# A 48-chunk FFT, feed-forward and soft-MoE kernel: first two chunks replanned, spare products added, last part written in order

## The chip, the core and the metric

One core of a Trainium2 chip runs the whole program. The metric is the device time of one execution in microseconds; three runs of the kernel before took 1926.4 to 1935.65 us, with a median of 1929.36.

## What is computed

Three stages, on 8 batches of 3072 tokens with 256 channels:

```python
X = np.fft.rfft(x, axis=1)
Y = X * (filt_r + 1j * filt_i)[None, :, :]
x = np.fft.irfft(Y, n=3072, axis=1).reshape(24576, 256)
h = x @ w_in                              # 256 -> 2048, float64 weights
g = h * (1.0 / (1.0 + np.exp(-h)))
x = g @ w_out                             # 2048 -> 256, float64 weights
logits = x @ phi                          # 32 slots: 8 experts of 4
d = softmax(logits, over all tokens); slot_input = d.T @ x
slot_out[e] = np.maximum(slot_input[e] @ w1[e], 0) @ w2[e]
c = softmax(logits, over the slots);  out = c @ slot_out
```

## The kernel before, in words

The tokens are worked in 48 chunks of 512, six to a batch. A chunk's path: `mat4` (products py) ends the inverse transform, `out4` splits the result into two parts yT, `hidden` makes 16 tiles ph of six products each with the split weights w_hl, `act` applies silu into a tile g, `turn` transposes g on DVE into X, `logits` multiplies g with wp (w_out times phi, folded once) into pl, a running softmax follows (`soft0` to `soft3`), the exponentials go through DRAM (`spread0`, `spread1`) and `dsum` (pd) adds the chunk's weighted sums, which `update` folds into acc on DVE. There are 12 buffers for g, so a hidden tile needs the turn and the logits of the tile twelve before it.

The transform of a batch is four steps: stage one (pa, twelve pairs of rows, stored to DRAM scratch s1), four visits Q of stage two (gather a from s1, products px, scaling with the filter f on ACT, DVE and POOL) and of stage three (pb, copied to eb and stored to scratch s2), from which each chunk loads b (`load3`), and `fly` makes bp on DVE. Batch 0 does this alone at the start (`first_plan`, L407 on), the others between the hidden tiles of the batch before (`fft_plan`, L262 on).

The weights w_in and w_out come as float64 words and are decoded on the chip in quarters q of 512 columns: `dec_act` on ACT, `dec_dve` and `dec_low` on DVE, and for w_in `split_act` and `split_dve`, for w_out `dec_move` on ACT. Quarter q of w_in serves hidden tiles 4q to 4q+3. `make_wp` (pw) and `put_wp` fold a quarter of w_out with phi into four of the sixteen slices of wp.

The order of nearly all instructions on every engine is set by hand: each call is entered with a number, `at(t, fn, ...)`, and the calls are written out in the order of these numbers, one unit being a sixteenth of a chunk. In `first_plan` the numbers are given in microseconds, `us(t) = (t - T0) / 1.42`. The number decides order only; an instruction starts when its engine reaches it and its inputs are there. Every engine works its own list in order. All DMAs are issued by SP's queue. What follows the last chunk (from L879: merging the sums, the experts, the output) is left to a scheduler.

After the last chunk, the sums are merged (ptot, pn), turned (pnt), multiplied by w_out (psi, pT), sent through the experts (peh, pht, pso), and the slot outputs are spread over the tokens (po, copied to ots and stored). The weights of six of the eight experts are loaded meanwhile into buffers that the main loop gives back.

Of the kernel before, what the change touches and what calls it, by code (L numbers as in the profile page):

```python
# [9 lines left out]
F32 = mybir.dt.float32  # L10
# [20 lines left out]
T0 = 74  # L31

# [10 lines left out]
def fftconv_moe_softmoe(ctx, tc, x, cmat, chl, dmat, emat, gmat, filt, filt0, sign, w_in, w_outT, w_out,  # L43
# [129 lines left out]
    def fill_rest(b, Q):  # L173
        for g in range(2):
            DQ.dma_start(s1t[b][g, Q, :, :, NJ:S].rearrange("q u r e -> (q u) (r e)"),
                         filt[4:6, 0:16].rearrange("a p u c e -> p a (u c e)"))
# [85 lines left out]
    def fft_plan(b, t0):  # L262
# [7 lines left out]
        def load1(u):  # L270
            t = fp.tile([P, 2, CH], F32, tag="ld", bufs=BUFS["ld"], name=f"x_{b}_{u}")
            DQ.dma_start(t, pair(xb, u))
            c = fp.tile([P, 2, P] if b == 1 else [P, 2, 2, P], F32, tag="c", bufs=BUFS["c"], name=f"c_{b}_{u}")
            DQ.dma_start(c, (cmat if b == 1 else chl)[:, 2 * u:2 * u + 2])
            ld[u] = (t, c)
# [95 lines left out]

        if b == 1:
            t1, tx = [11.7 + 0.95 * u for u in range(12)], t0 + 27.1
        else:
            t1, tx = [t0 + d for d in (-4.3, -3.1, -1.9, -0.7, 2.6, 4.2, 6.4, 8, 11.5, 12.6, 13.7, 14.8)], t0 + 27.1
        at(t1[0] - 10, begin)
        if b == 1:
            for Q in range(4):
                at(8 + 2 * Q, fill_rest, 1, Q)
# [9 lines left out]
        tp = tx  # L389
        for Q in range(4):  # L390
            t = tx if Q == 0 else t0 + 16 * Q + VIS1 + 16
            at(t1[-1] + 4 if Q == 0 else tp + 2, load2, Q)
            at(t + 0.004, mat2, Q)
            for U in range(4):
                at(t - 6 + U, loadf, Q, U)
                at(t + ((1, 1.4, 2.4, 2.8) if Q == 0 else (1.75, 2.25, 4.15, 5.15))[U], act2, Q, U)
                at(t + (0.25, 0.65, 1.45, 2.05)[U], direct2, Q, U)
                at(t + ((1.4, 2, 3, 4) if Q == 0 else (2.25, 2.75, 5.15, 6.15))[U], cross2, Q, U)
                at(t + ((3.6, 3.7, 6, 6.1) if Q == 0 else (4.1, 4.2, 8.3, 8.4))[U], add2, Q, U)
            t = t0 + 16 * Q + VIS1 + 32  # L400
            at(t, mat3, Q)
            at(t + 0.001, out3, Q)
            at(t + 0.15, store3, Q)
            tp = t - 16 + 0.004 if Q else tx


    def first_plan():  # L407
# [10 lines left out]
        def load(v):  # L418
# [4 lines left out]
            DQ.dma_start(cs[v], cmat[:, 4 * v:4 * v + 4, :])  # L423
# [85 lines left out]

        at(us(-5), begin)  # L510
# [3 lines left out]
        at(us(-2.9), load_small)  # L514
        for u in range(12):
            t = 6 + u + (1 if u else 0)
# [3 lines left out]
        for u, n, t in ((0, 4, 13.4), (4, 4, 17), (8, 2, 18.9), (10, 2, 20.6)):  # L520
            at(us(t), store1, u, n)
        for Q in range(4):
            at(us((18, 18.1, 22.01, 22.41)[Q]), fill_rest, 0, Q)
            at(us(22 + 0.4 * Q), load2, Q)
            for U in range(4):
                at(us(22.05 + 0.4 * Q + 0.1 * U), loadf, 4 * Q + U)
            t = 28 + 4.8 * Q
# [14 lines left out]
        for q, (t0, t1, t2, t3, t4, t5, t6) in enumerate(((5, 21, 21.1, 21.15, 21.2, 21.3, 21.4), (39, 52.3, 52.4, 52.5, 53, 53.5, 54), (48.5, 54.1, 55, 56, 56.2, 57, 57.1), (53, 77.5, 79.2, 79.3, 80, 85, 85.2))):  # L542
            at(us(t0), load_words, "in", q)
            at(us(t1), dec_act, "in", q, "a" if q % 2 == 0 else "xh")
            at(us(t2), dec_dve, "in", q, 0)
            at(us(t3), dec_dve, "in", q, 1)
            at(us(t4), dec_low, "in", q)
            at(us(t5), split_act, q)
            at(us(t6), split_dve, q)
        at(us(62.6), load3, 0)  # L550
        at(us(68.5), fly, 0)
        at(us(66.1), start)
        for q, t in enumerate((81, 84.5, 89, 92)):
# [214 lines left out]

    tail = {"w1": [], "w2": [], "t": []}
# [66 lines left out]
    for c in range(NCHUNK):  # L836
        t0 = 16 * c
        if c > 0:
            at(t0 - 16 + 6.9, loadd, c)
            at(t0 - 16 + 5.6, load3, c)  # L840
            at(t0 - 16 + 9.6 if c > 1 else 15, fly, c)
        ty = t0 - 16 + (VIS3 + 0.003 if c > 1 else 15.7) if c else -2
# [3 lines left out]
        for m in range(NM):  # L846
# [16 lines left out]
        at(t3 + 0.001, update, c)  # L863
        if c % 4 == 3:
            last = c == NCHUNK - 1
            at(t3 + 4 if last else t1 + (11.2 if (c + 1) % CPB else 19.1), cprep, c // 4)
            if last:
                at(t1 + 0.5, exp_table)
                at(t3 + 5, cexp, c // 4)
                at(t3 + 6, cfin, c // 4)  # L870
            else:
                at(t1 + {1: 43.8, 3: 27.8, 5: 19.1}[(c + 2) % CPB], cfin, c // 4)
# [263 lines left out]
```

## Time and profile before

| what | value |
|---|---|
| median of three runs | 1929.36 us |
| profiled execution: its own time, and its span | 1931.86 us, 1930.1 us |
| PE busy, share of the span | 1817.5 us, 94% |
| DVE, ACT, POOL busy | 1258.0, 952.2, 264.5 us |
| mean granted clock of PE | 0.971 |
| bytes moved by DMA, mean rate | 292.67 MB, 152 GB/s |
| first product of chunk 0 (py), start | 80.53 us |
| first product of the output (po), start | 1862.62 us |

The span runs from the first to the last instruction. A busy PE is not a PE at its peak: the granted clock says at which share of 2.4 GHz it ran. In rows below, L62 is the helper that issues nearly all products, so tiles tell them apart.

### The profile page before, as it was taken

The numbers are of one execution on the slowest core, as the hardware profiler recorded it, in microseconds if no ns is written. First come the engines' busy times: TensorE is split into PE (matmuls) and PEld (weight loads), VectorE is DVE, ScalarE is ACT, GpSimd is POOL, SyncE is SP. The second block draws the span as 40 slices with busy tenths as digits, with TensorE's granted clock in tenths as the row PEclk, the third lists the DMA queues.
The fourth block names the chain that finished last, engine by engine and source line by source line (L and its number), as shares of the span: only waits on it lengthen the run. The fifth ranks groups of instructions, "written<-read, shape, count | busy, mean of one in ns | idle before, by whom it ended". The sixth has DMA issues, their size and how long they took to land. (4 is left out here: it accounts for less than half of the span.)

```text
span 1930.1 us, 49986 instructions
## 1 busy us (share of the span) xinstructions
PE 1817.5 (94%) x21250; PEld 1372.7 (71%) x21250; DVE 1258.0 (65%) x2170; ACT 952.2 (49%) x1785; POOL 264.5 (14%) x200
## 2 busy tenths in 40 slices
PE   4588999999999999999999999999999999999884
PEld 2366777877787777777787778777787777777543
DVE  4685675676676765676676766677576766765433
ACT  2443645545554545455455556456455454443322
POOL 0201211121121211121121212122022110000000
PEclk7798999999999999999999999999999999999987
DMA  9935525543344515543354415444355413122669
GB/s 307 367 113 176 156 69 160 175 141 109 117 159 147 168 51 167 175 133 120 115 161 156 153 47 180 162 134 135 101 172 173 126 63 102 68 83 76 228 233 386
DMA packets 237038, 292.67 MB, mean 152 GB/s; under 512 B 19344, under 2 KB 177424, under 8 KB 236816
## 3 DMA queue, kind: packets, MB, share of 16 engines
q1 hardware_dynamic: 236816, 289.49, 45.7%
q8 instruction: 167, 2.74, 0.6%
q14 instruction: 55, 0.45, 0.1%
HBM read 199.82 MB, written 91.68 MB: 151 GB/s over the span
## 5 line engine op out<-in xcount | busy, mean ns | idle before, releaser
L62 PE MATMUL ph<-yT,w_hl 128*128 128x512 f32 x4608 | 1100.6, 394 | 2.2 <-ACT g L631 1.8
L62 PEld LDWEIGHTS ph<-yT,w_hl 128*128 128x128 f32 x4608 | 853.2, 189 | 207.6 <-issue 26.6
L641 DVE STREAM_TRANSPOSE X<-g 128x512 f32<-128x512 f32 x768 | 516.7, 695 | 214.7 <-ACT g L631 211.0
L631 ACT ACTIVATE g<-ph 128x512 f32<-128x512 f32 x768 | 454.6, 608 | 342.2 <-PE ph L62 294.0
L239 POOL TENSOR_TENSOR sw<-sw,f 128x512 f32<-128x512 f32 x124 | 170.7, 1401 | 864.6 <-DVE X L641 487.2
L609 ACT ACTIVATE yT<-py 128x512 fp32r<-128x512 f32 x96 | 57.4, 598 | 352.6 <-PE py L62 352.6
L62 PE MATMUL pd<-X,E 32*32 32x512 f32 x6144 | 220.3, 603 | 0.0
L62 PEld LDWEIGHTS pl<-g,wp 128*32 128x32 f32 x6144 | 163.1, 110 | 74.3 <-issue 49.4
L62 PE MATMUL pl<-g,wp 128*32 128x128 f32 x6144 | 189.8, 275 | 6.8 <-issue 3.5
L62 PEld LDWEIGHTS pd<-X,E 32*32 32x32 f32 x6144 | 115.5, 103 | 78.2 <-issue 42.7
L725 DVE SCALAR_TENSOR_TENSOR acc<-acc,nm,pd 128x512 f32<-128x512 f32 x188 | 127.7, 741 | 51.3 <-PE pd L62 51.2
L284 POOL TENSOR_TENSOR xh<-x,xh 128x512 fp32r<-128x512 f32 x72 | 93.5, 1299 | 436.9 <-DVE xh L283 427.4
L610 DVE TENSOR_TENSOR yT<-py,yT 128x512 fp32r<-128x512 f32 x96 | 66.3, 691 | 67.3 <-ACT yT L609 67.3
L357 DVE TENSOR_TENSOR y<-y,sw 128x512 f32<-128x512 f32 x112 | 103.8, 966 | 0.0
L62 PE MATMUL py<-d,b 128*128 128x128 f32 x416 | 66.3, 283 | 18.0 <-DMA b<-s 14.4
L236 DVE TENSOR_TENSOR y<-px,f 128x512 f32<-128x512 f32 x120 | 78.0, 676 | 6.5 <-PE px L62 5.5
L228 ACT ACTIVATE sw<-px,sg 128x256 f32<-128x256 f32 x124 | 62.7, 505 | 37.5 <-DVE y L234 32.1
L671 ACT ACT_TABLE_LOAD x48 | 61.6, 1283 | 37.0 <-DVE nm L664 27.0
L62 PE MATMUL px<-a,em 24*32 24x512 f32 (+1 forms) x1072 | 50.1, 628 | 24.3 <-DMA a<-s 23.3
L367 ACT ACTIVATE eb<-pb 128x512 f32<-128x512 f32 x112 | 57.8, 602 | 27.8 <-PE pb L62 27.8
L62 PEld LDWEIGHTS py<-d,b 128*128 128x128 f32 x416 | 56.4, 197 | 20.8 <-DMA b<-s 15.3
L62 PE MATMUL py<-d,bp 128*128 128x128 f32 x352 | 60.2, 291 | 9.9 <-DVE bp L592 6.1
(142 smaller groups left out, 1196.3 us busy)
## 6 DMA issues: line engine op xcount, KB each, us to landing
a<-s SPq DMA_DIRECT2D x64, 512.0 KB, 5.1
f<-in_filt_dram SPq DMA_DIRECT2D x128, 256.0 KB, 4.0
s<-eb SPq DMA_DIRECT2D x64, 512.0 KB, 4.1
x<-in_x_dram SPq DMA_DIRECT2D x96, 256.0 KB, 3.8
b<-s SPq DMA_DIRECT2D x160, 128.0 KB, 3.1
out_dram<-ots SPq DMA_DIRECT2D x40, 512.0 KB, 5.4
c<-in_chl_dram SPq DMA_DIRECT2D x72, 256.0 KB, 3.7
s<-ea SPq DMA_DIRECT2D x56, 256.0 KB, 3.7
```

The source lines that it names most:

```text
L62: T.matmul(o, lhsT=l, rhs=r, start=start, stop=stop)
L228: A.activation(sw[:, 0, :], p[:, 1, :], AF.Copy, scale=sg[:, s:s + 1])
L236: V.tensor_tensor(y, p, f[:, 0, :].unsqueeze(1).to_broadcast([P, 2, CH]), op=ALU.mult)
L239: G.tensor_tensor(sw, sw, f[:, 1, :].unsqueeze(1).to_broadcast([P, 2, CH]), op=ALU.mult)
L284: G.tensor_tensor(h[:, 1, :], tf, h[:, 0, :], op=ALU.subtract)
L357: V.tensor_tensor(y, y, st.pop(("sw", Q, U)), op=ALU.add)
L367: A.activation(st["eb"][:, q], p, AF.Copy)
L610: V.tensor_tensor(y[:, half, 1, :], py, y[:, half, 0, :], op=ALU.subtract)
L631: A.activation(g, pht.pop((c, m)), AF.Silu)
L641: V.transpose(xt[c][:, m].rearrange("p b j -> p (b j)"), gt[c, m])
L671: A.activation(t[:, 0], L, AF.Exp, bias=nm[:, 1:2], accum_out=nm[:, 2:3])
L725: V.scalar_tensor_tensor(out=acc[:, :, a, :], in0=acc[:, :, a, :], scalar=mrun[c][:, 3:4], in1=p, op0=ALU.mult, op1=ALU.add)
```

## The change

- **First transfers.** The six loads of cmat for batch 0 are issued by ACT instead of SP. Two quarters of w_in (before: one) are loaded ahead of stage one's stores, the third ahead of the stores of stage three, the fourth behind the first load of b. Stage one of batch 0 is stored in three groups of four rows (before: 4, 4, 2, 2). The filling of unused scratch rows is one transfer per Q, and one for all of batch 1.
- **Decoding.** The second quarter of w_in is decoded during stage two of batch 0, and the others and w_out have new places. The turns of chunk 0 from tile 4 on move into the time of chunk 1, those of chunk 1 are a little later, and the logits of chunk 0 stand at tile 11.6.
- **Batch two.** Stage one of batch 1 is spread between tiles of chunk 1 (before: 0 and 1), and its visits of stage two and three move from 27.1, 33.9, 49.9, 65.9, 81.9 to 33.9, 44.4, 53.4, 65.9, 81.9 units; its c tiles are loaded in pairs.
- **Spare products.** `keep(n)` multiplies a 128x128 tile with itself n times into a PSUM tile that nothing reads: 12 before stage one, 72 after it, 44 after stage three (all on fold, zeroed first), 9 and then 1 to 4 at a time in the last part (on the identity).
- **Last part.** It is written in a fixed order in `finish`. The last chunk's sums are not folded into acc: they are copied to SBUF as part and multiplied with fs, and acc with fo (fs times the rescaling), into the same pn. Exp's table is loaded before the last logits, `cprep` and `cexp` stand behind sim, `cfin` behind the second expert tile, and the turns of hr run one tile ahead.

```diff
+W_IN = ((-2.8, 20), (-2.75, 27.5), (21.8, 56), (59.5, 72))
+W_OUT = ((61.1, 76.7), (61.12, 79.5), (61.3, 90.5), (61.4, 94.2))
...
+        v1 = [t0 + 16 * i + VIS1 for i in range(6)]
         if b == 1:
-            t1, tx = [11.7 + 0.95 * u for u in range(12)], t0 + 27.1
+            t1 = [16.2 + 0.87 * u for u in range(12)]
+            tx, tb = (v1[2], t0 + 44.4, t0 + 53.4, v1[4]), (t0 + 44.4, t0 + 53.4, v1[4], v1[5])
+            at(13, fill_rest, 1)
...
-            DQ.dma_start(cs[v], cmat[:, 4 * v:4 * v + 4, :])
+            A.dma_start(cs[v], cmat[:, 4 * v:4 * v + 4, :])
...
+        at(us(-5), V.memset, fold, 0.0)
+        at(us(-4.5), keep, 12, fold)
...
+        at(us(-2.7), fill_rest, 0, 0)
         for u in range(12):
-            t = 6 + u + (1 if u else 0)
+            t = 6 + u
             at(us(t), mat1, u)
             at(us(t + 1.2), out1, u)
             at(us(t + 2), sums1, u)
-        for u, n, t in ((0, 4, 13.4), (4, 4, 17), (8, 2, 18.9), (10, 2, 20.6)):
-            at(us(t), store1, u, n)
+            if u % 4 == 3:
+                at(us(t + 2.2), store1, u - 3, 4)
+        at(us(18.5), keep, 72, fold)
...
+            at(us(t0), load_words, "in", q)
+            at(us(t1), dec_act, "in", q, "a" if q % 2 == 0 else "xh")
+            at(us(t1 + 1.2), dec_dve, "in", q)
+            at(us(t1 + 4.6), dec_low, "in", q)
+            at(us(t1 + 7), split_act, q)
+            at(us(t1 + 8.2), split_dve, q)
+        at(us(60), keep, 44, fold)
...
+            at((11.5, 11.55, 17.75, 17.8)[q], make_wp, q)
+            at((11.51, 11.56, 17.76, 17.81)[q], put_wp, q)
...
+    def keep(n, a=None):
+        t = ps_h.tile([P, P], F32, tag="ph", name="keep")
+        a = idt if a is None else a
+        for _ in range(n):
+            mm(t, a, a, True, True)
...
-            at(max(t + 1.45 if m not in (1, 10) else t + 0.8996, 0 if c else 12 + 0.3 * m), turn, c, m)
+            at(max(t + 1.45 if m not in (1, 10) else t + 0.8996, (16.6 + 0.8 * (m - 4) if m > 3 else 11.7, 17.9 + 0.2 * m)[c] if c < 2 else 0), turn, c, m)
...
+        if c == NCHUNK - 1:
+            at(t1 + 0.0025, keep, 9)
...
+        fo = tp.tile([P, S], F32, tag="fo", name="fo")
+        V.tensor_scalar(fo, fs, nm[:, 3:4], None, op0=ALU.mult)
+        parts = []
+        for a, p in enumerate(pdt.pop(NCHUNK - 1)):
+            parts.append(wk.tile([P, NM, 32], F32, tag="g", bufs=BUFS["g"], name=f"part_{a}"))
+            if a % 2:
+                V.tensor_copy(parts[a], p)
+            else:
+                A.activation(parts[a], p, AF.Copy)
+        pn = ps_1.tile([P, 512], F32, tag="pl", name="pn")
+        for g in range(4):
+            mm(pn[S * g:S * g + S], fo, acc[:, 4 * g:4 * g + 4].rearrange("p m a j -> p (m a j)"), True, False)
+        keep(2)
+        for a in range(4):
+            for g in range(4):
+                mm(pn.rearrange("p (m a j) -> p m a j", a=4, j=32)[S * g:S * g + S, :, a, :], fs,
+                   parts[a][:, 4 * g:4 * g + 4], False, a == 3)
...
+        turn_hidden(0)
+        for i in range(4):
+            r, n = divmod(i, 2)
+            if i < 3:
+                turn_hidden(i + 1)
```

SP's queue after the loads of x for batch 0, before the change: words_in is a quarter of w_in, s<-a a store of stage one, s<-in_filt_dram a fill, a<-s the gather of stage two.

```order
L94 DMA words_in<-in_w_in_dram 128x1024 x2
L198 DMA s_0_88<-a_126 64x4x256 x8
L175 DMA s_0_88<-in_filt_dram 16x2x1024 x4
L198 DMA s_0_88<-a_126 64x2x256 x8
L202 DMA a_126<-s_0_88 128x4x256 x2
L175 DMA s_0_88<-in_filt_dram 16x2x1024 x2
L452 DMA f_0_235<-in_filt_dram 128x512
```

And in the changed kernel:

```order
L96 DMA words_in<-in_w_in_dram 128x1024 x4
L178 DMA s_0_89<-in_filt_dram 16x2x2048
L202 DMA s_0_89<-a_140 64x4x256 x12
L178 DMA s_0_89<-in_filt_dram 16x2x2048
L458 DMA f_0_306<-in_filt_dram 128x512
L227 DMA f_0_308<-in_filt_dram 128x256
L458 DMA f_1_310<-in_filt_dram 128x512
L206 DMA a_140<-s_0_89 128x4x256 x2
```

Twenty transfers of stores and fills stood between the words and the first gather, and now fourteen, with four loads of words and three filter loads around them.

SP's queue at the end of stage three of batch 0, before: s<-eb are its stores, b<-s the load of chunk 0, acc<-in_w_in_dram the fourth quarter of w_in.

```order
L567 DMA d_277<-in_dmat_dram 128x512
L260 DMA s_0_89<-eb_0_405 128x4x256 x2
L94 DMA words_in<-in_w_in_dram 128x1024 x2
L260 DMA s_0_89<-eb_1_491 128x4x256 x2
L260 DMA s_0_89<-eb_2_577 128x4x256 x2
L94 DMA words_in<-in_w_in_dram 128x1024 x2
L260 DMA s_0_89<-eb_3_626 128x4x256 x2
L94 DMA acc<-in_w_in_dram 128x1024 x2
L579 DMA b_656<-s_0_89 64x768 x2
L579 DMA b_656<-s_0_89 64x256 x2
L94 DMA a_126<-in_w_outT_dram 128x1024 x2
```

And now:

```order
L96 DMA words_in<-in_w_in_dram 128x1024 x2
L578 DMA d_358<-in_dmat_dram 128x512
L264 DMA s_0_90<-eb_0_498 128x4x256 x2
L264 DMA s_0_90<-eb_1_582 128x4x256 x2
L264 DMA s_0_90<-eb_2_668 128x4x256 x2
L264 DMA s_0_90<-eb_3_716 128x4x256 x2
L590 DMA b_729<-s_0_90 64x768 x2
L590 DMA b_729<-s_0_90 64x256 x2
L96 DMA acc<-in_w_in_dram 128x1024 x2
L96 DMA a_140<-in_w_outT_dram 128x1024 x8
```

No words of w_in stand between the stores of eb any more, and the fourth quarter has moved behind b.

ACT's list around the two copies of yT for chunk 0 (db_in<-... is `dec_act`, w_hl<-words_in is `split_act`), before:

```order
L105 ACTIVATE db_in_631<-words_in 128x1024
L131 ACTIVATE w_hl<-words_in 128x2x512
L105 ACTIVATE db_in_646<-words_in 128x1024
L131 ACTIVATE w_hl<-words_in 128x2x512
L609 ACTIVATE yT_685<-py_0_675 128x512
L609 ACTIVATE yT_685<-py_1_680 128x512
L631 ACT_TABLE_LOAD
L631 ACTIVATE g_0_697<-ph_0_690 128x512
L631 ACTIVATE g_1_708<-ph_1_699 128x512
L105 ACTIVATE db_in_717<-acc 128x1024
```

And now:

```order
L107 ACTIVATE db_in_723<-words_in 128x1024
L133 ACTIVATE w_hl<-words_in 128x2x512
L620 ACTIVATE yT_809<-py_0_799 128x512
L107 ACTIVATE db_in_812<-acc 128x1024
L620 ACTIVATE yT_809<-py_1_804 128x512
L642 ACT_TABLE_LOAD
L642 ACTIVATE g_0_828<-ph_0_821 128x512
L642 ACTIVATE g_1_839<-ph_1_830 128x512
L107 ACTIVATE db_out_841<-a_140 128x1024
L642 ACTIVATE g_2_854<-ph_2_843 128x512
L133 ACTIVATE w_hl<-acc 128x2x512
```

The decoding of the second and third quarters stood directly ahead of the first copy; now the fourth quarter's start stands between the two copies, and its split ahead of g of tile 3.

## Rows read from the trace of the kernel before

**Rows 1.** The page: busy time by engine, and granted clock in 40 slices.

```profile
PE 1817.5 (94%) x21250; PEld 1372.7 (71%) x21250; DVE 1258.0 (65%) x2170; ACT 952.2 (49%) x1785; POOL 264.5 (14%) x200
...
PEclk7798999999999999999999999999999999999987
```

**Rows 2.** Windows: length, busy by engine (instructions), granted clock, DMA share, GB/s.

```profile
0.00:10.00 10.00, 4.46 (x11) 3.55 (x12) 0.17 (x1) 2.35 (x3) 0.20 (x4) 1.00 0.71 226
10.00:20.00 10.00, 9.36 (x39) 6.82 (x37) 8.52 (x20) 4.44 (x10) 0.00 (x0) 1.00 1.07 374
20.00:30.00 10.00, 0.00 (x0) 0.00 (x0) 7.38 (x10) 2.54 (x3) 0.00 (x0) 0.71 0.93 318
30.00:40.00 10.00, 2.99 (x36) 1.25 (x38) 0.94 (x1) 0.00 (x0) 0.00 (x0) 0.50 0.77 256
80.00:90.00 10.00, 5.40 (x20) 4.46 (x20) 5.75 (x8) 2.82 (x4) 0.00 (x0) 0.54 0.96 334
90.00:194.00 104.00, 90.26 (x884) 68.74 (x898) 70.12 (x113) 46.13 (x78) 5.07 (x4) 0.92 0.49 157
```

**Rows 3.** Waits of PE: total us, times, longest.

```profile
PE py L62 <- DVE bp L592: 6.1, 2, 4.1
```

**Rows 4.** Timeline of SP's queue, first 100 us: start, us, line, transfers issued.

```profile
16.32 6.27 SPq L198 DMA_DIRECT2D s<-a  x8
...
25.76 5.27 SPq L198 DMA_DIRECT2D s<-a  x8
32.55 0.94 SPq L202 DMA_DIRECT2D a<-s  x2
...
67.62 1.39 SPq L260 DMA_DIRECT2D s<-eb  x2
...
75.67 3.19 SPq L579 DMA_DIRECT2D b<-s  x4
```

**Rows 5.** Timeline of PE, first 160 us: start, us, operation, records, idle before.

```profile
17.82 1.97 PE L62 MATMUL pa<-x,c 128*128 128x256 f32 x8 [0.22 <-DVE a L191]
36.59 1.03 PE L62 MATMUL px<-a,em 24*32 24x256 f32 x2 [16.80 <-DMA a<-s]
...
64.44 1.74 PE L62 MATMUL pb<-sw,gm 32*32 32x512 f32 x29
80.53 0.79 PE L62 MATMUL py<-d,b 128*128 128x128 f32 x2 [14.36 <-DMA b<-s]
...
90.25 15.71 PE L62 MATMUL ph<-yT,w_hl 128*128 128x512 f32 x68 [0.23 <-DVE yT L610]
...
159.40 4.49 PE L62 MATMUL pd<-X,E 32*32 32x512 f32 x128
```

**Rows 6.** Groups on DVE between 88 and 140 us: count, busy, mean ns.

```profile
L641 DVE STREAM_TRANSPOSE X<-g 128x512 f32<-128x512 f32 x17 | 11.1, 686 | 1.3 <-PE pw L62 1.3
L114 DVE SCALAR_TENSOR_TENSOR db_out<-a,db_out 128x1024 uint32<-128x1024 uint32 x4 | 4.9, 1226 | 0.1
```

**Rows 7.** Groups on ACT between 88 and 140 us: count, busy, mean ns.

```profile
L631 ACT ACTIVATE g<-ph 128x512 f32<-128x512 f32 x18 | 10.6, 602 | 10.3 <-PE ph L62 6.8 <-PE pl L62 2.9 <-issue 0.6
...
L128 ACT ACTIVATE a<-db_out 128x1024 f32<-128x1024 f32 x4 | 4.6, 1162 | 3.8 <-DVE db_out L114 3.8
```

**Rows 8.** Timeline of PE in the last part: start, us, operation.

```profile
1821.92 6.52 PE L62 MATMUL pd<-X,E 32*32 32x512 f32 x128
...
1834.68 4.23 PE L62 MATMUL psi<-wo,nT 128*32 128x256 f32 x32 [0.53 <-ACT nT L941]
...
1853.70 1.93 PE L62 MATMUL pso<-wt,hT 128*32 128x256 f32 x32 [0.25 <-ACT hT L974]
...
1862.62 7.79 PE L62 MATMUL po<-so,cl 32*128 32x256 f32 x104 [0.52 <-DVE so L983]
```

**Rows 9.** Timeline of DVE in the last part.

```profile
1828.28 2.72 DVE L725 SCALAR_TENSOR_TENSOR acc<-acc,nm,pd 128x512 f32<-128x512 f32 x4 [5.56 <-PE pd L62]
```

**Rows 10.** Timeline of ACT in the last part.

```profile
1818.13 1.28 ACT L671 ACT_TABLE_LOAD   x1 [0.77 <-DVE nm L664]
```

More of the change, by code (lines that the diff above doesn't have):

```diff
@@ L171, in scratch, with fill_rest @@
         return s1t[b % 2], s2t[b]
[L173 to L176, printed above, removed]
+    def fill_rest(b, Q=None):
+        to = s1t[b] if Q is None else s1t[b][:, Q:Q + 1]
+        n = 64 if Q is None else 16
+        DQ.dma_start(to[:, :, :, :, NJ:S].rearrange("g k q u r e -> (k q u) g (r e)"),
+                     filt[4:4 + n // 32 + 1].rearrange("a p u c e -> (a p u c e)")[0:n * 4096]
+                     .rearrange("(n g e) -> n g e", n=n, g=2))
     def pair(a, u):
@@ L840, in fftconv_moe_softmoe @@
             at(t0 - 16 + 5.6, load3, c)
[L841 to L842 removed]
+            at(t0 - 16 + 9.6 if c > 1 else 11.6, fly, c)
+        ty = t0 - 16 + (VIS3 + 0.003 if c > 1 else 14.9) if c else -2
         for h in range(2):
@@ L862, in fftconv_moe_softmoe @@
         at(t3, dsum, c)
-        at(t3 + 0.001, update, c)
+        if c < NCHUNK - 1:
+            at(t3 + 0.001, update, c)
         if c % 4 == 3:
             last = c == NCHUNK - 1
-            at(t3 + 4 if last else t1 + (11.2 if (c + 1) % CPB else 19.1), cprep, c // 4)
             if last:
-                at(t1 + 0.5, exp_table)
-                at(t3 + 5, cexp, c // 4)
-                at(t3 + 6, cfin, c // 4)
+                at(t0 + 16.95, exp_table)
             else:
+                at(t1 + (11.2 if (c + 1) % CPB else 19.1), cprep, c // 4)
                 at(t1 + {1: 43.8, 3: 27.8, 5: 19.1}[(c + 2) % CPB], cfin, c // 4)
@@ L906, in w2_of @@
-    def w2_of(e, k):
-        return w27[k // 2][:, k % 2, :] if e == 7 else w2t[e][:, k, :]
-    t = wk.tile([P, 16, TC], F32, tag="X", bufs=BUFS["X"], name="cl")
-    for k in range(NK - 2):
-        cl[k] = t[:, k, :]
-        DQ.dma_start(cl[k], cT[k])
-    nm = mrun[NCHUNK - 1]
-    mg = tp.tile([P, 8], F32, tag="mg", name="mg")
-    for a in range(4):
-        V.tensor_copy(mg[0:S, a:a + 1], nm[a * S:a * S + S, 0:1])
-    V.tensor_reduce(mg[0:S, 4:5], mg[0:S, 0:4], axis=AX.X, op=ALU.max)
@@ L929, in fftconv_moe_softmoe @@
-    V.tensor_scalar(fs, fold[:, 0:S], mg[:, 6:7], rec[:, 0:1], op0=ALU.mult, op1=ALU.mult)
-    pn = ps_h.tile([P, 512], F32, tag="ph", name="pn")
-    for g in range(4):
-        mm(pn[S * g:S * g + S], fs, acc[:, 4 * g:4 * g + 4].rearrange("p m a j -> p (m a j)"), True, True)
-    ns = wk.tile([P, 512], F32, tag="E4", bufs=BUFS["E4"], name="ns")
-    A.activation(ns[:, 0:256], pn[:, 0:256], AF.Copy)
-    V.tensor_copy(ns[:, 256:512], pn[:, 256:512])
-    pnt = ps_h.tile([P, 4, P], F32, tag="ph", name="pnt")
@@ L968, in fftconv_moe_softmoe @@
-    for i in range(4):
-        r, n = divmod(i, 2)
-        pt = ps_f.tile([P, 4, P], F32, tag="pf", name=f"pht_{i}")
-        for k in range(4):
-            T.transpose(pt[:, k, :], hr[i][:, k * P:k * P + P], idt)
-        t = wk.tile([P, 4, P], F32, tag="g", bufs=BUFS["g"], name=f"hT_{i}")
-        A.activation(t, pt, AF.Copy)
-        for k in range(4):
-            for g in range(4):
-                mm(pso[S * g:S * g + S], t[:, k, S * g:S * g + S], w2_of(4 * r + g, 4 * n + k), i + k == 0, i + k == 6)
@@ L1017, in _dft @@
+    with tc.manual_schedule(engines={E.PE, E.SP, E.Activation, E.DVE, E.Pool}):
+        finish()
 def _dft():
```

290 lines of the change are left out of this document (159 added, 131 removed).

## Prediction

> **What bounds the kernel now.** I read the page first: PE is busy for 94% of the span and its clock is full from the fifth slice to near the end, but granted at less in the first four slices and the last three [rows 1]. So the middle can give nothing; what the change can move lies before about 194 us and after the last hidden products. I then cut the first part into windows and followed the two queues that set it.
>
> Up to the first product of chunk 0 (py_0 at 80.53 us) it is the transfers. The DMA engines move 374 GB/s when full and only 226, 318 and 256 in the windows 0:10, 20:30 and 30:40 [rows 2]. The hole at 20 to 36 us comes from SP's queue: eight stores of stage one issue from 16.32, four fills and eight smaller stores follow until 31.03, and the first gather a<-s can start only at 32.55, after the last store has landed [rows 4]; PE gets its first stage-two product at 36.59, having waited 16.80 us [rows 5]. At the other end the last store of stage three issues at 67.62 and the load of b that needs it at 75.67, with a quarter of w_in queued on either side [rows 4]; PE waits 14.36 us [rows 5], and then 4.1 us more because the fly products on DVE stand behind a decoding [rows 3].
>
> From 90 to 194 us PE is the engine that should be full and is not: 90.26 us busy of 104, so 13.7 us idle, and a mean clock of 0.92 [rows 2]. With two levels, 1.2 and 2.4 GHz, 0.92 means 16% of the stretch, 16.6 us, at the lower one, and half of that, 8.3 us, lost. So 22 us can be had there at most.
>
> In the last part a chain runs through PE, DVE and ACT until po starts at 1862.62 [rows 8]; behind it only the stores of the output, about as long as before whatever happens ahead of them.
>
> **The change, part by part.** *First transfers.* Bytes queued ahead of py_0 fall by one quarter of w_in: the fourth quarter now stands behind b. That is 1 MiB, or 1.05 MB / 374 GB/s = 2.8 us. The sixteen stores of stage one become twelve, no fill but one stands ahead of them, and a second quarter of w_in fills the queue in their place. The hole in 20:40 is (374-318) x 10 + (374-256) x 10 = 1.74 MB, 4.7 us of transfer; I expect a<-s to land at about 36 again, since the extra words (1 MiB) pass ahead of it, with 1.3 MB more moved by then, 3.5 us, and take 3.7 with the start. Bounds: 0, if the stores land as late as now and the words only push them, and 4.7. Sum for py_0: 6.5 us, so about 74.0.
>
> The loads of cmat go to ACT's queue, six issues that no longer stand among SP's. ACT's first work on data is after the first stage-one product, so they cost nothing there; without that cover they would cost ACT some 3 us. The Trainium skill, "DMA: Bandwidth & Descriptors", section "Issuing engines are not separate DMA queues", says that transfers started by several engines share the same 16 DMA engines and only issue time is saved. The 226 GB/s of window 0:10 agrees that issue is short there, but by that rule this edit alone gives only what lies in that window.
>
> *Spare products.* A 128x256 fp32 product takes 1.97 / 4 = 0.49 us at full clock [rows 5], so one of 128x128 about 0.25; the trace has none of these back to back, and I bound one by 0.25 and 0.49 (lower clock). Twelve are over in 3 us, before x_0 lands. Seventy-two follow the last pa product, which ends at 19.8 now and near 19 then: 18 us, until about 37, just when a<-s lands. Forty-four follow the last pb product, which ends at 66.2 now [rows 5] and near 63 then: 11 us, until 74. PE's queue is in order, so px and py wait for them; as sized they end with the data. What they buy is the clock: 0.50 in 30:40 and 0.54 in 80:90 [rows 2].
>
> *From py_0 to the first hidden tile.* The decoding of the second quarter moves to the idle DVE of 20 to 40 us, and the third's is over before b lands, so the 4.1 us wait for bp goes [rows 3]. The clock gives back about 2.4 us of the py and the first hidden products, issued at 0.54. Against that, ACT now decodes the fourth quarter between its two copies of yT, and that quarter lands 2.8 us behind b: 2.3 us of new wait, with the second half of yT on DVE and all hidden products queued behind it. Net 4.2 us, bounds 0 and 6.5. Hidden tile 0 (six products of 15.71 / 68 = 0.231 us [rows 5]) would end at 80.0 instead of 90.7 (two of its products stand in that row): **10.7 us**.
>
> *Chunks 0 and 1.* Of the 22 us lost in 90:194, the plan removes the waits for batch two's first visit (its products come one visit later, with their gather long landed), for d, and for logits behind turns. The turns of chunk 0 now spread over chunk 1; 12 of them at 0.686 us [rows 6] leave the DVE queue ahead of the second decoding of w_out. I walked the new queues with durations of rows 6 and 7 and find waits left: 1.7 us where hidden tile 10 needs the copy of tile 6, which stands behind two 1.16 us moves on ACT; 0.5 before pw, 0.5 before the logits, 1.1 before the fourth pw (its decoding ends last on DVE); 1.7 at dsum of chunk 0, which needs the last turn. That is 5.5. Two later visits now run pb and px back to back with no logits between, so px waits for three copies of pb on ACT, 0.6 us each: 3.5 for both. So 9 of 22 stay: **13 us**. Bounds: 0 (the same DVE work, only shifted) and 19.
>
> *Last part.* Exp's table load (1.28 us [rows 10]) comes before the logits are there: 1.0. The last dsum takes 6.52 us where a warm one takes 4.49 [rows 8, 5]: 2.0. The update of acc (2.72 us on DVE [rows 9]) becomes four copies shared by two engines and sixteen short products; with cprep no longer ahead of the copy of ns: 1.7. psi takes 4.23 us against 1.93 for the pso of equal size at full clock [rows 8]: 2.2. The expert products, partly at the lower clock like psi: 1.5, an estimate from psi's ratio. Turning hr one step ahead hides three copies of 0.6 us [rows 7]: 1.7. Together 10.1. But one half expert (1 MiB) that was loaded early now loads in line, 2.8 us, and the third expert tile may wait for it: 3 back. **7 us**, bounds 3 and 10.
>
> Sum: 10.7 + 13 + 7 = 30.7. The profiled execution took 1931.86 us (span 1930.1, 1.8 around it), so 1901.2; the median of the three timed runs is 2.5 lower, which would give 1898.7. I say **1900**. Everything else in the diff (fills in one transfer, c in pairs, the part without a scheduler) I cost at nothing: the fills and c of batch two run at a DMA share of 0.49 in 90:194 [rows 2].
>
> **Rivals.** *The decoding still rules.* DVE must decode four quarters of w_out and one of w_in whatever the order, and PE, earlier by 10.7 us, would only wait longer for wp. Speaking for it: decodings of 1.23 us a pass [rows 6] on one engine in order. Against: the turns left its way. Then the 13 us shrink to 0: 1914.
>
> *The transfers don't shrink.* py_0 at 80, since the words pushed ahead of the stores use up the hole; the first term is 4.2 and the second DVE-limited at 6: 1931.9 - 4.2 - 6 - 7 = 1915, and with a tail held by the weights (3) 1919.
>
> *PE runs chunks 0 and 1 at the lower clock.* The one that ends on the other side. The Trainium skill, "TensorE: Matmul & The Clock Gate", section "HAM oscillation — how this bites in real kernels", says that repeated idle gaps throttle the clock again each time. Here the mechanism would be: many short waits between hidden tiles and pa products, paced by DVE, hold the clock at 1.2 GHz; each microsecond of PE work at that level costs one more. From 31 us of such work on, the gain is gone; from 41 on it is slower by 0.5%; all of chunk 1, about 50 us with its pa products, gives 1950. Against it: the worst stretch now, with waits of all kinds in it, has 0.92 [rows 2].
>
> *All is better than walked:* no clock lost, tail 10, 17 in the chunks: 1892.
>
> **How the numbers follow.** Forecast 0.60, decoding 0.17, transfers 0.09, low clock 0.04, better 0.10. The forecast's own spread is 1892 to 1908 from its bounds taken together. The range 1886 to 1917 leaves out the slow clock, the worst of the transfers and the extreme of the better case, somewhat under 2 in 10. A change of 0.5%, 9.6 us, is about what this kernel's measurement can tell from none (its three runs span 1926.4 to 1935.65). Faster than 1919.7: 0.88; within: 0.08, from the worse ends of the two middle rivals; slower: 0.04.
>
> **What would show it.** In the changed trace: py_0 near 74 and hidden tile 0 ending near 80; a<-s landing near 36 as the spare products end; clock 1.00 in 20:90 except between px products; a window like 90:194, shifted, with under 10 us lost; dsum of chunk 0 near 141 instead of 159.40 [rows 5]; po some 7 us sooner after the last logits than now. I am wrong if px or py wait for the spares' end by several microseconds, if wp comes after hidden tile 11 by more than 3 us, or if expert tiles wait for weights.

## The result, and the profile after

The changed kernel takes **1906.3 us**, the median of four runs (1903.02 to 1915.53); the kernel before takes 1929.22 beside it (1926.4 to 1935.65). The ratio is 0.9885, with a 95% interval of 0.9863 to 0.9908: faster by 1.15%. The profiled execution took 1908.89 us, 22.97 less than that of before. Where these 23 us came from is read at marks that both traces have, with the same work done by PE ahead of each (the dsum of chunk 1 is left out, since before had done more of batch two's px and pb by then):

| mark | before | after | gain so far |
|---|---|---|---|
| first product py_0 starts | 80.53 | 77.36 | 3.2 |
| hidden tile 0 ends | 90.7 | 84.4 | 6.3 |
| dsum of chunk 0 starts | 159.40 | 148.15 | 11.3 |
| dsum of chunk 2 | 241.89 | 223.76 | 18.1 |
| dsum of chunk 3 | 276.35 | 262.82 | 13.5 |
| last logits end | 1817.02 | 1801.85 | 15.2 |
| po starts | 1862.62 | 1839.22 | 23.4 |
| end of the span | 1930.1 | 1907.1 | 23.0 |

So: 6.3 us up to tile 0, 11.8 more up to chunk 2, 4.6 lost behind it, 1.7 found again over the other chunks, 8.2 in the last part, and 0.4 lost in the output (from po's first product to the end of the span).

The page after, to be read beside [rows 1]: PE is busy for 29 us more, but 38 us of its time are spare products now (16.2, 10.1 and 5.4 in the first part, 6.4 in the last), so busy time is no measure of work here. The clock is full nearly everywhere.

```profile
PE 1846.2 (97%) x21582; PEld 1402.8 (74%) x21582; DVE 1259.1 (66%) x2170; ACT 952.6 (50%) x1787; POOL 266.6 (14%) x200
...
PEclk9899999999999999999999999999999999999997
```

Windows of after (length, busy by engine, granted clock, DMA share, GB/s), beside [rows 2]:

```profile
0.00:10.00 10.00, 7.57 (x33) 6.71 (x34) 0.17 (x1) 1.88 (x2) 0.20 (x4) 1.00 0.77 251
20.00:30.00 10.00, 10.00 (x90) 9.95 (x89) 8.51 (x12) 3.56 (x5) 0.00 (x0) 1.00 1.06 384
30.00:40.00 10.00, 8.47 (x96) 7.39 (x96) 3.67 (x5) 0.27 (x1) 0.00 (x0) 1.00 0.92 312
40.00:50.00 10.00, 4.76 (x62) 1.73 (x67) 9.12 (x13) 3.95 (x9) 5.32 (x3) 0.52 1.06 376
70.00:80.00 10.00, 9.62 (x84) 9.24 (x82) 6.93 (x8) 1.73 (x2) 0.00 (x0) 1.00 0.72 225
80.00:90.00 10.00, 7.88 (x27) 5.55 (x26) 7.35 (x9) 6.02 (x9) 0.00 (x0) 0.83 1.02 403
```

The same window 70:80 of before:

```profile
70.00:80.00 10.00, 0.00 (x0) 0.00 (x0) 8.61 (x9) 2.15 (x2) 0.00 (x0) 0.50 0.99 374
```

The hole in the transfers at 20 to 40 us is filled for the greater part (384 and 312 GB/s where there were 318 and 256), and a new one has opened at 70 to 80 us (225 where there was 374). SP's queue after, beside [rows 4]:

```profile
17.88 10.74 SPq L202 DMA_DIRECT2D s<-a  x12
...
33.23 0.93 SPq L206 DMA_DIRECT2D a<-s  x2
...
56.55 12.55 SPq L264 DMA_DIRECT2D s<-eb  x8
72.57 3.21 SPq L590 DMA_DIRECT2D b<-s  x4
```

The first gather leaves at 33.23 (before 32.55) and the last store of stage three is out at 56.55 + 12.55 = 69.10 (before 67.62 + 1.39 = 69.01): no gain up to there. The gain is behind it: b is issued 3.5 us after that store and not 6.7. What the stores of stage three wait for on SP between 50 and 80 us (total us, times, longest) is above all the copies of pb into eb on DVE, and 2.6 us for those on ACT:

```profile
SPq L264 <- DVE eb L511: 7.3, 3, 2.8
```

PE's timeline after, beside [rows 5]; the bracket is the idle time before a row and what ended it:

```profile
20.34 16.24 PE L64 MATMUL keep<-fold 128*128 128x128 f32 x144
37.38 0.59 PE L64 MATMUL px<-a,em 24*32 24x256 f32 x2 [0.80 <-DMA a<-s]
...
46.28 2.73 PE L64 MATMUL px<-a,em 24*32 24x512 f32 x29 [5.24 <-DMA a<-s]
...
67.44 10.09 PE L64 MATMUL keep<-fold 128*128 128x128 f32 x88 [0.69 <-ACT eb L509]
77.36 0.39 PE L64 MATMUL py<-d,b 128*128 128x128 f32 x2
...
83.19 0.50 PE L64 MATMUL ph<-yT,w_hl 128*128 128x512 f32 x1 [1.66 <-ACT yT L620]
83.91 17.66 PE L64 MATMUL ph<-yT,w_hl 128*128 128x512 f32 x68 [0.22 <-DVE yT L621]
```

The spares end as their data land, to within a microsecond; px starts 0.8 us later than before; the 1.66 us wait for yT is the forecast one, where ACT decodes the fourth quarter between its two copies. Tile 0 ends two products (0.26 us each) into the last row, at 84.4. Further on, PE's timeline at batch two's visits and at the dsum of chunk 2:

```profile
195.24 2.96 PE L64 MATMUL px<-a,em 24*32 24x512 f32 x32
...
213.58 3.18 PE L64 MATMUL px<-a,em 24*32 24x512 f32 x32
...
223.76 4.39 PE L64 MATMUL pd<-X,E 32*32 32x512 f32 x121
230.15 1.06 PE L64 MATMUL pd<-X,E 32*32 32x512 f32 x7 [2.00 <-issue]
```

A px takes 3 us where it stands right behind pb, as forecast. The 2.00 us ahead of the last seven products of pd are time in which PE waited for no other engine and no transfer of data (see the last section); they are the 4.6 us lost behind chunk 2 together with what follows at a lower clock (0.50 in 232:235). The last part, beside [rows 8]:

```profile
1804.95 1.04 PE L64 MATMUL pd<-X,E 32*32 32x512 f32 x2 [0.35 <-ACT E L713]
...
1806.23 4.45 PE L64 MATMUL pd<-X,E 32*32 32x512 f32 x126
...
1815.78 2.30 PE L64 MATMUL psi<-wo,nT 128*32 128x256 f32 x32
...
1839.22 9.62 PE L64 MATMUL po<-so,cl 32*128 32x256 f32 x128 [0.52 <-DVE so L1031]
```

From the end of the last logits to po it is 37.4 us where it was 45.6.

### The profile page after: what moved, and what is told of

Read it like the earlier page. It is cut to its first block, busy times and chain, and to the rows that moved or that the text cites. A ratio compares the mean times of both kernels' runs of the same rounds, so it can differ in the third digit from the quotient of the medians.

```text
span 1907.1 us, 50623 instructions
## 1 busy us (share of the span) xinstructions
PE 1846.2 (97%) x21582; PEld 1402.8 (74%) x21582; DVE 1259.1 (66%) x2170; ACT 952.6 (50%) x1787; POOL 266.6 (14%) x200
## 3 DMA queue, kind: packets, MB, share of 16 engines
q10 hardware_dynamic: 864, 1.57, 0.2%
## 5 line engine op out<-in xcount | busy, mean ns | idle before, releaser
L232 ACT ACTIVATE sw<-px,sg 128x256 f32<-128x256 f32 x124 | 62.4, 503 | 29.6 <-DVE y L238 12.6
L64 PEld LDWEIGHTS pa<-xh,ch 128*128 128x128 f32 x432 | 61.3, 189 | 5.8
L233 ACT ACTIVATE sw<-px,sg 128x256 f32<-128x256 f32 x124 | 63.3, 511 | 0.0
L64 PE MATMUL pa<-xh,ch 128*128 128x256 f32 x432 | 62.9, 282 | 0.0
```

What stands on the lines that cost most here:

```text
L64: T.matmul(o, lhsT=l, rhs=r, start=start, stop=stop)
L232: A.activation(sw[:, 0, :], p[:, 1, :], AF.Copy, scale=sg[:, s:s + 1])
L233: A.activation(sw[:, 1, :], p[:, 0, :], AF.Copy, scale=sg[:, s + 1:s + 2])
```

## The experiments

A median below stands with its own ratio to the kernel before, timed on the same chip. Runs of one kernel spread by up to 12 us and more, so most small edits are read at the marks. In the kernels that don't touch the start, px starts between 36.95 and 37.84 and py between 77.17 and 79.08.

**1. The last part alone.** The kernel before with the new `finish`, its first spares, exp's table earlier and no update for the last chunk; the first part untouched.

> The kernel before with the new last part alone (its finish, its nine spare products, the earlier table of exp, no update for the last chunk). Theory: the two halves of the change are independent, and the last part gives the 8.2 us by which the stretch from the last logits to po was shorter in the trace after (37.4 us against 45.6): about 1921 us, 8 less than before, and the same 37.4 us in that stretch. Rival: the last part is only fast because the first part left weights or buffers earlier; then the stretch is over 40 us long and the gain under 5 us.

1922.62 us against 1931.47, ratio 0.9954 (0.9939 to 0.9968): 8.9 less, and 37.3 us from the last logits to po. So the last part gives the same with the old first part ahead of it, and by difference the first part is worth the other 14 us.

**2. No spares in the last part.**

```diff
-            at(t1 + 0.0025, keep, 9)
...
-        keep(2)
```

> The changed kernel without the 22 spare products of its last part. Theory: those products keep the clock at 1.00 there, which I priced at 2.2 us for psi and 1.5 for the expert products: the stretch from the last logits to po grows from 37.4 us to about 40, psi from 2.30 to some 4.2 us, and the time by 2 to 3 us. Rival: the gain came from the shorter chain alone (table load, warm dsum, no update); then the stretch stays within 1 us of 37.4.

1908.63 us, ratio 0.988 (0.9864 to 0.9897), and 37.5 us from the last logits to po. PE's timeline of this run:

```profile
1804.26 6.11 PE L64 MATMUL pd<-X,E 32*32 32x512 f32 x128
...
1814.16 2.38 PE L64 MATMUL psi<-wo,nT 128*32 128x256 f32 x32 [0.52 <-ACT nT L971]
```

The theory falls. pd is slow again (6.11 us) and ends 0.8 us later after the logits, but psi starts 0.5 sooner, with no spares in the chain, and takes 2.38 us without any of them, where it took 4.23 before the change. The likely reason, not tried alone, is that the 2.6 us wait for the update ahead of psi in the trace of before is gone.

**3. No spares in the first part** (the 12, 72 and 44 taken out).

> The changed kernel without the 12, 72 and 44 spare products of the first part. Theory: transfers set when py starts, and the spares buy the clock only: px starts at about 36.5 as a<-s lands (0.8 us sooner), py at 76 to 77 when b lands, and py and the first hidden products then run at the lower clock, so that hidden tile 0 ends about 1 to 2 us later than 84.4; the whole time goes up by 1 to 4 us (also from the px products between 37 and 47). Rival: the 44 spares hold py back; then py starts at 74 or before without them, hidden tile 0 ends no later than 83, and the time is 1 us less or more.

1910.56 us (1901.76 to 1913.79), ratio 0.9887 (0.9858 to 0.9917). PE's timeline of this run:

```profile
77.54 0.77 PE L64 MATMUL py<-d,b 128*128 128x128 f32 x2 [9.60 <-DMA b<-s]
...
84.54 13.03 PE L64 MATMUL ph<-yT,w_hl 128*128 128x512 f32 x56 [0.23 <-DVE yT L618]
```

b lands at 77.5 with PE idle, so the spares do not hold py. Without them a py or ph takes about twice as long until 83 us, and tile 0 ends at 85.0, 0.6 later; the dsum of chunk 0 starts at 147.26, 0.9 sooner. They buy half a microsecond, which is gone by chunk 0's end. The windows show where it goes. With spares the clock is high at py and falls at 85 us, behind the 1.66 us wait for yT, while the hidden products run; without them it is full again from 84 us on. First the changed kernel, then this run:

```profile
85.00:88.00 3.00, 3.00 (x8) 2.31 (x7) 2.90 (x4) 1.25 (x3) 0.00 (x0) 0.50 1.02 418
```

```profile
86.00:90.00 4.00, 4.00 (x19) 3.27 (x19) 3.90 (x4) 2.15 (x3) 0.00 (x0) 1.00 1.02 415
```

**4. The fourth quarter of w_in ahead of the last store of stage three.**

```diff
-W_IN = ((-2.8, 20), (-2.75, 27.5), (21.8, 56), (59.5, 72))
+W_IN = ((-2.8, 20), (-2.75, 27.5), (21.8, 56), (53, 72))
```

> The changed kernel with the fourth quarter of w_in ahead of the last store of stage three, as in the kernel before, and its decoding where the change has it. Theory: that one quarter (1 MiB, 2.8 us at 374 GB/s) behind b is the whole of what py won: b lands 2.8 us later, py at about 80 instead of 77.4, and the time is 1 to 3 us up, less what the earlier fourth quarter saves on ACT and DVE. Rival: the last store of stage three is late because of PE's products and not of transfers, and the words fit into the hole of 70 to 80 us (225 GB/s there); then py stays within 1 us of 77.4.

1911.07 us, ratio 0.9896 (0.9876 to 0.9917). The theory holds: PE's timeline has

```profile
80.40 0.71 PE L64 MATMUL py<-d,b 128*128 128x128 f32 x2 [2.68 <-DMA b<-s]
```

3.0 us later than 77.36, b is issued at 76.21 and not 72.57, and the dsum of chunk 0 at 151.09 is 2.9 later. Within the spread of py, that one quarter accounts for the 3.2 us that py gained. (In the kernel before, it stood one place later in SP's queue, between the last store and b.)

**5. The second quarter of w_in behind the gathers.** Two runs; the first left its decoding where it stood, and ACT, in order, stopped stage two for words that had not landed.

```diff
-W_IN = ((-2.8, 20), (-2.75, 27.5), (21.8, 56), (59.5, 72))
+W_IN = ((-2.8, 20), (21.7, 33.5), (21.8, 56), (59.5, 72))
...
-        at(us(18.5), keep, 72, fold)
+        at(us(18.5), keep, 52, fold)
```

> The changed kernel with the second quarter of w_in loaded behind three of the four gathers of stage two, as it no longer stands ahead of the stores of stage one (with 52 spare products instead of 72, so that PE is free when the gather lands). Theory: the words that fill the hole of 20 to 40 us stand in the stores' way, and so the hole was filled with nothing won: here px starts at 34 to 35 instead of 37.4 and its second part at 43 to 44 instead of 46.3, while the bytes ahead of b are the same, so that py stays within 1.5 us of 77.4. Rival: the stores of stage one are late because of PE and DVE and not of the words; then px stays at 36.5 or later and py comes 1 to 3 us later than 77.4, as the hole is open again.

1923.16 us, ratio 0.9964 (0.995 to 0.9978). px starts at 34.92 as the theory says, but then waits behind the decoding, and py comes at 94.88, so this run tells only of px. Waits of PE:

```profile
PE px L64 <- ACT sw L233: 11.7, 1, 11.7
```

The second run decodes both middle quarters behind stage three: `(21.7, 54), (21.8, 59)`.

> As the run with the second quarter of w_in behind three gathers, but with its decoding on ACT and DVE behind the last product of stage three, so that ACT does not stop for it in stage two (and 52 spares instead of 72). Theory: the words ahead of the stores of stage one are what keeps px at 37.4; here px starts at 34.5 to 35.5, its second part at 43 to 44.5 instead of 46.3, and the last pb product ends at 64 to 65.5 instead of 66.7; then b is issued 1.5 to 3 us before 72.57, unless the quarter that now passes in 45 to 60 us, where the engines are full, holds the stores of stage three as long as it held those of stage one (b at 72 to 74). Rival for py: with two decodings (13 us of DVE) behind stage three it waits for DVE and starts at 79 or later whatever b does.

1910.92 us, ratio 0.9907 (0.9887 to 0.9927). SP's queue of this run:

```profile
30.53 0.93 SPq L206 DMA_DIRECT2D a<-s  x2
...
56.39 15.94 SPq L264 DMA_DIRECT2D s<-eb  x8
74.51 3.29 SPq L590 DMA_DIRECT2D b<-s  x4
```

The first gather leaves at 30.53 and not 33.23: 2.7 us, about one quarter at 374 GB/s (2.8). The spread is wide, but does not reach that far: 31.80 to 33.69 in the kernels with both quarters in front, 30.53 and 30.73 in the two runs here. px starts at 34.96, and its second part at 43.09 (46.28). But the last pb product ends at 66.57, no sooner than 66.74 and outside the theory's 64 to 65.5, the last store is out at 72.33 and not 69.10, b leaves 1.9 us later, and py starts at 78.99.

The late store does not come from the words. SP's wait ahead of it, and what it waits for on DVE:

```profile
SPq L264 <- DVE eb L511: 7.3, 2, 6.5
```

```profile
70.05 0.69 DVE L117 TENSOR_SCALAR de_in<-db_in 128x1024 uint32<-128x1024 uint32 x1
70.66 0.68 DVE L511 COPY eb<-pb 128x512 f32<-128x512 f32 x1
```

The last copy of pb stands on DVE behind four passes of the second quarter's decoding (from 67.35 on), and the DMA engines are all but idle meanwhile (23 GB/s in 70:72). So the 1.9 us at b and the 1.6 at py tell of the place of that decoding. What the run shows is that words ahead of stage one's stores delay the gather by about their own transfer time. What filling the hole is worth at b it can't tell; against the order of before it moved the last store not at all (69.10 and 69.01).

**6. The decoding behind both copies of yT.**

```diff
-W_IN = ((-2.8, 20), (-2.75, 27.5), (21.8, 56), (59.5, 72))
+W_IN = ((-2.8, 20), (-2.75, 27.5), (21.8, 56), (59.5, 72.5))
```

> The changed kernel with the fourth quarter of w_in decoded behind both copies of yT on ACT. Theory: the wait of the hidden products for yT (1.66 us on ACT in the trace after) goes, and the first hidden tile ends at 82.0 to 82.8 where it ended at 84.4; but the fourth quarter is then ready later by one pass of 1.1 us, and as every hidden product needs all of w_hl, what is won on yT may be lost on w_hl; 1.5 us less in the whole time if not. Rival: the first hidden product's later half waits for the fourth quarter anyway, and hidden tile 0 ends at 84 to 86, no gain.

1909.07 us, ratio 0.9886 (0.9866 to 0.9906). The wait goes and tile 0 ends at 82.0, 2.4 us sooner. PE's timeline shows it come back:

```profile
80.80 9.75 PE L64 MATMUL ph<-yT,w_hl 128*128 128x512 f32 x41 [0.22 <-DVE yT L621]
91.28 4.37 PE L64 MATMUL ph<-yT,w_hl 128*128 128x512 f32 x18 [0.72 <-ACT g L642]
97.31 3.01 PE L64 MATMUL ph<-yT,w_hl 128*128 128x512 f32 x12 [1.67 <-ACT g L642]
```

ACT, with the decoding moved among its silus, is late with g. A wait for g of 1.57 and 1.29 us stands in experiments 3 and 4 too, where the decoding has its old place, so ACT's pace takes back part of what comes sooner here. pw starts 1.2 us sooner, and the dsum of chunk 0 at 147.98, 0.2 sooner, since the loads of c then make up the rest (1.73 and 2.60 us of wait where there were 0.94 and 2.33).

**7. The turns of chunk 0 back ahead of the decoding.**

```diff
-... (16.6 + 0.8 * (m - 4) if m > 3 else 11.7, 17.9 + 0.2 * m)[c] if c < 2 else 0)
+... 0 if c else 12 + 0.3 * m)
```

> The changed kernel with the turns of chunk 0 where the kernel before had them, ahead of the second decoding of w_out on DVE. Theory: the spread of the turns over chunk 1 is what lets wp come in time; here twelve turns of 0.69 us come first again, so the third and fourth pw and the logits behind them come some 5 to 8 us later, PE idles there, and dsum of chunk 0 starts at 153 to 157 instead of 148.15, the whole time 4 to 8 us up. Rival: DVE has the same work in either order up to 145 us, and PE catches up where it now waits for loads of c at 136 to 142; then dsum of chunk 0 stays within 2 us of 148 and the time within 3.

1915.98 us, ratio 0.9933 (0.9908 to 0.9958): 9.7 more than with the turns spread. The dsum of chunk 0 starts at 157.62, just past the theory's range; 1.7 of the 9.5 us was there at py, and 0.7 at the end of tile 0. Timeline of PE:

```profile
117.14 2.32 PE L64 MATMUL ph<-yT,w_hl 128*128 128x512 f32 x5 [3.39 <-DVE yT L621]
...
128.00 3.40 PE L64 MATMUL pl<-g,wp 128*32 128x128 f32 x64 [1.09 <-DVE wp L156]
```

What is late first is yT of chunk 1, then wp, both behind turns on DVE, and the clock falls with the waits. From the end of tile 0 to the dsum of chunk 0 it is 72.5 us here, 63.7 in the changed kernel and 68.7 before. So the spread of the turns is worth 8.8 us there, and what else is new in that stretch takes 3.8 of it back. The other 6.9 of the 11.8 us are won between the dsums of chunk 0 and chunk 2 and do not hang on the turns (75.5 us in this run, 75.6 in the changed kernel, 82.5 before). There the kernel before waits, and the changed one does not; waits of PE before, 159 to 242 us:

```profile
PE px L62 <- DMA a<-s: 2.9, 2, 2.5
PE py L62 <- DMA d<-in_dmat_dram: 2.8, 1, 2.8
```

**8. px a hidden tile behind pb** at two of batch two's visits.

```diff
-            tx, tb = (v1[2], t0 + 44.4, t0 + 53.4, v1[4]), ...
+            tx, tb = (v1[2], t0 + 45.4, t0 + 54.4, v1[4]), ...
```

> The changed kernel with px of two of batch two's visits placed one hidden tile behind pb, where the change runs the two back to back. Theory: px waits there for the copies of pb on ACT and the clock pays too (2.96 and 3.18 us for px in the trace after, 1.14 us for a px with a tile between); the two visits win 3.5 us, dsum of chunk 1 to dsum of chunk 2 takes 37.9 us instead of 41.4, and the whole time is 3 us less. Rival: PE only meets the same wait at the hidden tile that follows, or the later px makes the next pb wait for its data; then 41 us again and no gain.

1908.32 us, ratio 0.9879 (0.9855 to 0.9903). The px products take 1.29 and 1.25 us, but from dsum to dsum it is 40.55 us where it was 41.38. The first visit wins 1.35; at the second, pb now has to wait for its data. PE's timeline of this run:

```profile
211.94 1.91 PE L64 MATMUL pb<-y,gm 32*32 32x512 f32 x24
214.06 1.06 PE L64 MATMUL pb<-y,gm 32*32 32x512 f32 x8 [0.22 <-DVE y L365]
```

The rival holds for three quarters of the 3.5 us.

**9. Batch two's loads from GpSimd's queue.** Three runs: alone, with the edit of 6 and that of 8 at the first visit only, and last with the same two edits and the loads moved only from the fourth tile of x on.

```diff
-            DQ.dma_start(t, pair(xb, u))
+            q = G if b == 1 else DQ
+            q.dma_start(t, pair(xb, u))
...
+            q = G if b == 1 and u > 2 else DQ
```

> The changed kernel with the loads of x and c of batch two's stage one issued from GpSimd's queue, which has no work between 66 and 172 us, instead of SP's. Theory: at 130 to 145 us SP is what holds PE: it waits for PE to free a tile of x (27.1 us in total between 90 and 160) and has stores, b and E behind that wait, and the next load of c behind those, so that PE waits 0.94 and 2.33 us for c and the clock falls to 0.78; with a queue of their own the loads land in time, these waits go, and dsum of chunk 0 starts at 144 to 146 instead of 148.15, the time 3 us less. Rival: DVE sets the pace there (4.9 of 5 us busy from 105 to 140), and PE only meets the wait at DVE's next result: dsum of chunk 0 stays within 1.5 us of 148.

1912.76 us, ratio 0.9915 (0.9888 to 0.9942). From py (80.18) to the dsum of chunk 0 (148.95) it is 2.0 us less, but the theory's 144 to 146 is missed: PE still waits 2.3 us for c (3.3 in the changed kernel), and the queue, free at 65 us, sends five loads at once, and b is issued 2.7 us later. The issues between 55 and 80 us:

```profile
x<-in_x_dram POOLq DMA_DIRECT2D x3, 256.0 KB, 7.0
c<-in_cmat_dram POOLq DMA_DIRECT2D x2, 256.0 KB, 6.2
```

> The changed kernel with three of the mendings together: the loads of batch two's stage one on GpSimd's queue, the fourth quarter of w_in decoded behind both copies of yT, and px one hidden tile behind pb at one visit (the one where that won 1.35 us). Theory: they add, since the first moves the wait at 136 to 142 us out of the way of what the second wins: dsum of chunk 0 at 142 to 145, dsum of chunk 2 some 5 us sooner than 223.76, and the time at about 1901. Rival: DVE is the pace of chunks 0 and 1, so that only the last of the three is left, 1 us, within the spread of the runs.

1907.33 us, ratio 0.9896 (0.987 to 0.9921): py again late (81.03), the dsum of chunk 0 at 150.15, where the theory had 142 to 145.

> The changed kernel with the fourth quarter of w_in decoded behind both copies of yT, px one hidden tile behind pb at one visit, and the loads of batch two's stage one on GpSimd's queue from the fourth tile of x on only, so that none of them moves before b has landed. Theory: the earlier run with all these loads on that queue lost 2.8 us at py because five of them ran while b waited, and won 2.0 us from py to dsum of chunk 0; here py stays at 77.4 to 78, dsum of chunk 0 starts at 145 to 146.5, dsum of chunk 2 at 220 to 221.5 (223.76 in the trace after), and the time is 1901 to 1904, about 3 us under the changed kernel. Rival: DVE's pace gives all back, dsum of chunk 0 stays at 148 and the time at 1906 to 1909.

1906.62 us (1902.58 to 1909.74), ratio 0.9875 (0.9855 to 0.9894); the profiled execution took 1904.34. At the marks the theory holds: py 77.17, the dsum of chunk 0 at 143.99 and that of chunk 2 at 220.25, 4.2 and 3.5 us sooner than in the changed kernel. PE still waits 2.2 us for c, so a queue of its own removes a third of that wait. One wait of 3.1 us in a late chunk, put down to d by the trace, took part of the rest. In the time, where the theory had 1901 to 1904, the rival's 1906 to 1909 came: it is not to be told from the changed kernel.

## Why the prediction was right, and where its steps were not

Forecast 1900 with 1886 to 1917, measured 1906.3: the forecast case came, with a gain of 23 and not 30.7.

- **First transfers: the failed step.** Of the 6.5 us, the 2.8 for one quarter behind b are right (3.0, experiment 4). The other term, "take 3.7 with the start" for the filled hole, measured nothing. The bytes did move as worked out: up to 69 us it is 24.09 MB where it was 22.67, 1.4 MB or 3.8 us. What was wrong is that the hole was taken for spare transfer time. It is the round trip from stage one's last store to the gather, and 1 MiB ahead of the stores made the gather 2.7 us later (experiment 5). From there a chain of px, pb and copies leads to the last store, which waits for the last copy and not for the queue; the time won stood idle again in the next round trip, 70 to 80 us. The prediction named this as its lower bound and then did not take it. py_0 came at 77.4, not 74.
- **py_0 to tile 0.** Right in kind: 7.1 us where it was 10.2, so 3.1 of the 4.2. The wait for bp is down to 0.35 us and the yT wait is there. The clock wins 1.8 us at py (2.7 us from its start to the first ph, 4.5 without spares), but the wait for yT takes most of that back: 0.6 is left at tile 0 of the 2.4 forecast, and nothing behind it, since the clock then falls (experiment 3).
- **Chunks 0 and 1: right in size**, 11.8 of 13, and in the mechanisms named: turns out of the way of decoding (8.8 us, experiment 7), and the waits for d and for batch two's first gather gone. Part of the size is luck. Of the 5.5 us of waits that the prediction walked through, none is in the trace; the loads of c, which it cost at nothing by the DMA share, stand in their place:

```profile
PE pa L64 <- DMA c<-in_cmat_dram: 3.3, 2, 2.3
```

  The mean share says little about an order in which SP waits for PE (27.1 us between 90 and 160). The two px behind pb take 2.96 and 3.18 us where 1.14 is usual, about the 3.5 forecast, but a tile between them wins back only 0.8 (experiment 8).
- **Last part: right in size** (8.2 for 7), because two errors cancel: the shares came to 8.2 and not 10.1, and the 3 us taken off for weights were not needed. Earlier table and warm dsum gave 2.6 of 3.0, the update 1.1 of 1.7, psi 2.1 of 2.2, the experts 0.7 of 1.5, hr 1.7 of 1.7, and no weights were waited for. That psi came down is not due to the spares (experiment 2).
- **cmat on ACT.** 251 GB/s in 0:10 where it was 226, and yet the first pa product starts at 6.62 (5.54) and the last ends at 20.51 (19.79). The rule cited from the Trainium skill ("DMA: Bandwidth & Descriptors", section "Issuing engines are not separate DMA queues") is that only issue time is saved. Nothing here speaks against it, but no run has this edit alone.
- **The rivals.** That decoding still rules, with nothing won in chunks 0 and 1, is excluded by the 11.8 us; experiment 7 shows that DVE's order does rule when the turns come first. The transfers shrank by less than half of what was said, so that rival was nearer than its 0.09. The low clock came in chunks 0 and 1 only for some 3 us each behind two waits, at 85 and at 143 us (0.50 in 85:88 and 143:146).

Of the gap of 7.7 us between 30.7 and 23.0, 4.4 lie ahead of tile 0, 1.2 in chunks 0 to 2, and 4.6 in the stall at chunk 2, against 1.2 more in the last part and 1.3 from the rest.

## What to carry to other kernels

An idle stretch of the DMA queues between a store and the load that reads it back is not free transfer time: here 1 MiB of loads put ahead of the store made the load that reads it back 2.7 us later, and 1 MiB moved behind the last transfer that PE waits for won 3.0. Before spare products are added for the clock, run the new order without them: psi took 2.30 us with spares, 2.38 without, and 4.23 in the old order. Gains are kept only where the next engine in the chain has slack: the waits taken away in experiments 6 and 8 came back to nine tenths and three quarters within a chunk. So read small edits at marks, and look for what moved in between, as the late copy of pb in experiment 5.

## What was not expected

**A stall between two fixed products.** In five of the twelve kernels that have the new first part (the changed one, and experiments 3, 8 and the first two of 9), PE stops between the 121st and the 122nd product of chunk 2's dsum for 2.0 to 3.7 us without waiting for another engine or for data; from dsum 2 to dsum 3 it is then 39.06 to 42.07 us, and 34.44 to 34.49 in the five that have none (experiments 2, 4, 6, 7 and the last). Both runs of 5 have a shorter one in the logits behind (0.83 and 1.36 us). The traces point to the program's own instructions, which come in transfers of 16 KB that the profile lists as kind instruction, queue q8. In the changed kernel, between 227.7 us and the stall's end:

```profile
q8 instruction: 1, 0.02, 2.4%
```

This transfer runs from 227.76 to 228.71 us, about 20 us after the one before it, and PE goes on at 230.15. In all seven kernels with a stall, the two of 5 included, PE goes on 1.3 to 1.4 us after such a transfer has ended. In the five without, such a transfer starts 4.5 to 7 us ahead of the 122nd product, and PE runs on; in experiment 6:

```profile
223.54 4.46 PE L64 MATMUL pd<-X,E 32*32 32x512 f32 x128
```

That the late transfer is the cause is read from this order in twelve traces and not from a run made for it. A busy DMA alone does not do it: between 227 and 229 us the engines move over 350 GB/s in the changed kernel and in experiment 6 alike. Why the transfer is late in some kernels and not in others was not tried and stays open. The stall is as large as most of the edits above, and makes 4.6 of the 7.7 us by which the profiled run falls short of the sum.

**Products of zeros hold the clock.** With 72 products of an all-zero tile the granted clock stays at 1.00 in 20:40, where it was 0.71 and 0.50 [rows 2]; the clock falls all the same at 40.5 us, behind waits of 0.80 and 0.73 us and among 36 px products of 24 rows, before the 5.24 us wait for the second gather begins at 41.0 (0.52 in 40:50).
